# The seam of two feed-forward stages: banks, sum tiles, token low parts and planned load times

## The chip, the cores and the metric

One core of one Trainium2 chip runs the whole program. The metric is the device time of one execution in microseconds (us), given as the median of several runs. The engines are named as in the profile: PE is TensorE (its weight loads are listed as PEld), DVE is VectorE, ACT is ScalarE, POOL is GpSimd, and SP is the engine whose queue issues the DMAs here.

## The reference, cut to what matters

```python
attn_out = _attn_ref(q, k, v, f)                 # 4 batches, 8 heads, 576 tokens, 64 per head
x = attn_out.transpose(0, 2, 1, 3).reshape(2304, 512)
h = x @ moe_w_in                                 # 512 -> 2048
x = (h * (1.0 / (1.0 + np.exp(-h)))) @ moe_w_out # 2048 -> 512: the first feed-forward stage
a, b = x @ moe2_w_a, x @ moe2_w_b                # 512 -> 1536, twice
return (a * b) @ moe2_w_out                      # 1536 -> 512: the second stage
```

All of it is float32. The change concerns the end of the first stage and the whole of the second.

## The kernel before

Each float32 operand of a product is split into a high part (rounded to fp32r, by ACT) and a low part (value minus high part, by DVE or POOL). A product is then three matmuls (high by high, high by low, low by high; `mm3`, lines 336 to 338).

Weights arrive as 64-bit words and are decoded on the chip by ACT, DVE and POOL (`fields`, lines 1069 to 1078). The hidden units of a stage are cut into chunks. The second stage has six chunks, numbered j, of 256 hidden units each. Its two first products (m = 0 for `w_a`, m = 1 for `w_b`) use a Strassen-like scheme of seven products (k = 0 to 6) in the place of eight, so `matrix` makes sums and differences of weight quarters (`ws`, `stage`, line 1102), whose high and low parts go to the weight tiles `whi` and `wlo` (lines 1107 and 968 or 969). `build` does the same for the tokens: plain quarters and differences (`t`, line 1054) of the first stage's result `acc`, their high parts (line 1057) and low parts (lines 968 on DVE, 969 on POOL) into `x`.

The tokens are cut into three blocks, each of two halves of 384. A chunk is run over the three blocks; one such pass is a "third" (`third(q)`, q = 0 to 17). In a third, PE forms products `x`, `y`, `z` in PSUM, ACT and DVE combine them to `z` tiles (lines 1169 to 1200), the product a*b is split into `ghi` and `glo`, and eight second products `po` are added to `acc` (line 1221, or 1219 by ACT for j = 0). The second products of a third are placed between the first products of the next one. Where j changes, the weights of the next chunk take the place of the old ones; the text calls that a change of chunk.

The last chunk of the first stage is `finish_first`: six token blocks of two first products `ps_l`, a gate (tiles `g_l`, `ghi_l`, `glo_l`; lines 991 to 996) and four second products `po_l`, added to `acc` by DVE (line 1007). The text calls the stretch from the first `ps_l` to the first `po` of the second stage the seam.

From the seam on, the order of all engines comes from a planner. `Plan.order` takes ready operations in order of start time and priority, with a cost per operation, and an engine then executes its list strictly in that order. A buffer belongs to a tag (a ring of slots), and the buffers of one tag are taken in the order in which the program adds them, so a tile can't be taken before an older one of its tag. `plan.dma(..., late)` says how late a transfer's users are planned. An operation with `also` may be planned on a second engine, when that one would end it 0.4 us earlier than the first. The tag `u` has seven slots, for the `z` tiles and for the sums of weights and tokens alike; PSUM has the tags `s` (four banks), `t` (two), `pv` and `mm` (one each).

## Time and profile before

| | |
|---|---|
| median of 3 runs | 1018.27 us (1016.64 to 1018.53) |
| the profiled execution, own time | 1019.05 us |
| its span, first to last instruction | 1017.3 us |
| mean granted TensorE clock | 0.996 |
| the seam in it | 530.6 to 611.3 us |
| the 18 thirds of the second stage | about 580 to 1013.6 us, overlapping the seam |

The span is that of the trace; the 1.75 us between it and the execution's own time lie outside the instructions. All positions in the text are us from the span's start.

### The profile page before, as it was taken

How to read it: one execution, taken by the hardware profiler on the slowest of the kernel's cores; microseconds unless marked ns; L12 is line 12 of the kernel's file. 1: busy time of each engine (PE TensorE's matmuls, PEld its weight loads, DVE VectorE, ACT ScalarE, POOL GpSimd, SP SyncE). 2: the span in 40 equal slices, each digit the busy share in tenths (PEclk: the TensorE clock that was granted, in tenths of full speed). 3: DMA queues.
4: the chain of work that ended last, by engine and by line, in shares of the span. 5: the costliest groups of instructions: out<-in, count | busy, mean ns of one | idle time of the engine just before them, and what ended most of it. 6: DMA issues, size and time to landing. Idle time of an engine off the chain costs nothing.

```text
span 1017.3 us, 17206 instructions
## 1 busy us (share of the span) xinstructions
PE 993.3 (98%) x6041; PEld 891.5 (88%) x6041; DVE 765.5 (75%) x1854; ACT 490.5 (48%) x1211; POOL 293.1 (29%) x366
## 2 busy tenths in 40 slices
PE   8999999999999999999999989999999999999998
PEld 7667777898888888888898989999999999999998
DVE  7885656749986856757869999967887897887545
ACT  6798888955434324323325457544333334343221
POOL 5674434424322403403313232221121131130000
PEclk9999999999999999999999999999999999999999
DMA  5443333122220201201203435272262441630523
GB/s 167 147 147 112 111 101 104 58 65 70 66 63 21 82 23 32 84 11 37 89 22 125 147 136 204 73 259 83 85 215 74 154 158 63 221 110 31 195 101 109
DMA packets 64022, 105.67 MB, mean 104 GB/s; under 512 B 8764, under 2 KB 40140, under 8 KB 63904
## 3 DMA queue, kind: packets, MB, share of 16 engines
q1 hardware_dynamic: 63824, 104.13, 31.8%
q8 instruction: 47, 0.77, 0.3%
q10 hardware_dynamic: 112, 0.45, 0.2%
q14 instruction: 39, 0.32, 0.1%
HBM read 87.51 MB, written 17.03 MB: 103 GB/s over the span
## 4 chain that ended last, share of the span: by engine, by line
PE 68%; DVE 9%; DMA 1%; issue 1%; ACT 0%; SPq 0%; DVEq 0%; ACTq 0%
PE po L336 9%; PE po L337 9%; PE po L338 9%; PE ps L337 5%; PE ps L336 5%; PE ps L338 5%; PE x L336 4%; PE x L338 4%; PE x L337 4%; PE z L336 2%; PE z L338 2%; PE z L337 2%; DVE wlo L968 1%; DVE ws L1102 1%; DMA d<-in_w 1%; PE y L336 1%
## 5 line engine op out<-in xcount | busy, mean ns | idle before, releaser
L336 PE MATMUL po<-ghi,whi 128*128 128x384 f32 (+2 forms) x528 | 184.0, 352 | 4.8 <-DVE acc L1221 4.5
L337 PE MATMUL po<-glo,whi 128*128 128x384 f32 (+2 forms) x528 | 184.7, 350 | 0.0
L338 PE MATMUL po<-ghi,wlo 128*128 128x384 f32 (+2 forms) x528 | 184.7, 350 | 0.0
L336 PEld LDWEIGHTS po<-ghi,whi 128*128 128x128 f32 x528 | 99.1, 188 | 15.4 <-DVE acc L1221 7.4
L337 PEld LDWEIGHTS po<-glo,whi 128*128 128x128 f32 x528 | 99.3, 188 | 7.6
L338 PEld LDWEIGHTS po<-ghi,wlo 128*128 128x128 f32 x528 | 99.3, 188 | 7.6
L1221 DVE TENSOR_TENSOR acc<-po,acc 128x384 f32<-128x384 f32 x120 | 66.1, 551 | 51.6 <-PE po L338 51.6
L1181 ACT CAST ghi<-z 128x384 fp32r<-128x384 f32 x72 | 37.0, 514 | 115.6 <-DVE z L1177 99.7
L336 PE MATMUL x<-x,whi 128*128 128x384 f32 x264 | 89.3, 338 | 2.7 <-DVE z L1175 1.7
L1087 POOL TENSOR_TENSOR stage<-d,d 128x256 f32<-128x256 f32 x40 | 31.9, 802 | 208.3 <-DVE d L1078 116.5
L337 PE MATMUL x<-x,whi 128*128 128x384 f32 x264 | 88.9, 337 | 0.0
L338 PE MATMUL x<-x,wlo 128*128 128x384 f32 x264 | 88.8, 336 | 0.0
L337 PE MATMUL ps<-x,whi 128*128 128x512 f32 (+1 forms) x240 | 88.4, 368 | 0.0
L336 PE MATMUL ps<-x,whi 128*128 128x512 f32 (+1 forms) x240 | 88.4, 368 | 0.0
L338 PE MATMUL ps<-x,wlo 128*128 128x512 f32 (+1 forms) x240 | 88.4, 368 | 0.0
L306 POOL TENSOR_TENSOR d<-d,whi 128x256 f32<-128x256 f32 x44 | 36.8, 840 | 145.5 <-ACT whi L305 119.6
L390 DVE SCALAR_TENSOR_TENSOR acc<-po,acc 128x512 f32<-128x512 f32 (+2 forms) x120 | 63.1, 550 | 18.9 <-PE po L338 18.6
L628 ACT ACTIVATE p<-p,nm 128x384 f32<-128x384 f32 (+3 forms) x128 | 70.7, 556 | 3.6 <-DVE nm L620 3.2
L620 DVE CUSTOM_DVE_ANT_0 p<-s,maskw 128x512 f32<-128x512 f32 (+3 forms) x128 | 55.8, 484 | 13.8 <-PE t_y L670 6.4
L546 POOL TENSOR_TENSOR qkl<-qk,qkh 128x304 fp32r<-128x304 f32 x60 | 48.6, 841 | 46.4 <-DVE qkh L542 31.0
L368 ACT CAST ghi<-g 128x512 fp32r<-128x512 f32 (+1 forms) x60 | 34.5, 576 | 40.0 <-DVE g L364 40.0
L363 ACT ACTIVATE g<-ps 128x512 f32<-128x512 f32 (+1 forms) x60 | 32.9, 549 | 42.8 <-PE ps L338 42.8
(214 smaller groups left out, 2635.9 us busy)
## 6 DMA issues: line engine op xcount, KB each, us to landing
x<-cache SPq DMA_DIRECT2D x80, 384.0 KB
d<-in_w SPq DMA_DIRECT2D x116, 256.0 KB
cache<-x SPq DMA_DIRECT2D x30, 384.0 KB
qk<-in_qk SPq DMA_DIRECT2D x15, 608.0 KB
vt<-in_v SPq DMA_DIRECT2D x16, 320.0 KB
out_t<-acc SPq DMA_DIRECT2D x24, 192.0 KB
rb<-invs SPq DMA_DIRECT2D x32, 128.0 KB
d2ghi<-in_w SPq DMA_DIRECT2D x8, 256.0 KB
```

Source lines behind the costliest of these rows:

```text
L306: nc.gpsimd.tensor_sub(m, val, hi.bitcast(F32))
L336: nc.tensor.matmul(ps, wh, mh, start=start, stop=False, skip_group_check=joined)
L337: nc.tensor.matmul(ps, wh, ml, start=False, stop=False, skip_group_check=joined)
L338: nc.tensor.matmul(ps, wl, mh, start=False, stop=stop, skip_group_check=joined)
L363: nc.scalar.activation(g, ps, AF.Tanh, scale=0.5)
L368: nc.scalar.copy(ghi[:, t, :n], g)
L390: nc.vector.scalar_tensor_tensor(a, ps, 0.5, a, ALU.mult, ALU.add)
L546: plan.add("POOL", t_pool(QK // 4), lambda c=c: nc.gpsimd.tensor_sub(lo()[:, c], raw()[:, c], hi().bitcast(F32)[:, c]), [(hi, "h"), raw], ...
L620: plan.add("DVE", t_dve(nj) + 13, lambda out=out, low=low, o=o, mk=mk: nc.vector.tensor_tensor_reduce(out(), o(), mk, -SCALE, 3.0e38, ALU. ...
L628: plan.add("ACT", t_act(sum(IB[ib]), 279), lambda b=b, c=c, nj=sum(IB[ib]): nc.scalar.activation(b()[:, :nj], b()[:, :nj], AF.Exp, bias=nm ...
L1181: plan.add("ACT", t_act(N2, 93), lambda: nc.scalar.copy(ghi()[:, t, h], z()), [z], [(ghi, t, h)], at)
L1221: plan.add("DVE", t_dve(N2), lambda ps=ps, a=a: nc.vector.tensor_add(a, ps()[:, :N2], a), [ps], [key], at + 2)
```

## The change

1. The four second products `po_l` of a block take the banks `t`, `t`, `pv`, `mm` in the place of `t` alone.
2. Sums of weights and tokens get a tag of their own, `sum`, with two slots.
3. `build` offers its low parts to POOL first and to DVE second, and goes through the columns c in the outer loop and the terms k in the inner one. All seven terms of block 1 are built in one call, and block 0 is built between the two weight matrices.
4. Loads of weights and of saved tokens are planned 2.5 us later.

```diff
-    SLOTS.update(u=7, g=2)
+    SLOTS.update(u=7, g=2, sum=2)
...
-    def low_part(dst, full, high, reads, writes, pr, n, deps=()):
-        plan.add("DVE", t_dve(n), lambda: nc.vector.tensor_sub(dst(), full(), high()), reads, writes, pr, port=True,
-                 also=[("POOL", t_pool(n), lambda: nc.gpsimd.tensor_sub(dst(), full(), high()))])
+    def low_part(dst, full, high, reads, writes, pr, n, first="DVE"):
+        ways = [("DVE", t_dve(n), lambda: nc.vector.tensor_sub(dst(), full(), high())),
+                ("POOL", t_pool(n), lambda: nc.gpsimd.tensor_sub(dst(), full(), high()))]
+        if first == "POOL":
+            ways.reverse()
+        plan.add(*ways[0], reads, writes, pr, port=True, also=ways[1:])
...
-                ps = bank2("t", f"po_l{i}_{oc}")
+                ps = bank2(("t", "t", "pv", "mm")[oc], f"po_l{i}_{oc}")
...
-                    [("cache", blk, k, i)], [(key, slot)], pr + k)
+                    [("cache", blk, k, i)], [(key, slot)], pr + k, late=2500)
...
-        for k in terms:
-            for c in range(2):
+        for c in range(2):
+            for k in terms:
...
-                    src = key = temps[k, c] = tbuf("u", [P, N2], F32, f"t_{blk}_{k}_{c}")
+                    src = key = temps[k, c] = tbuf("sum", [P, N2], F32, f"t_{blk}_{k}_{c}")
...
-                low_part(lo, src, lambda hi=hi: hi().bitcast(F32), [key, ("xh", st[k], c)], [("xl", st[k])], pr + k, N2)
+                low_part(lo, src, lambda hi=hi: hi().bitcast(F32), [key, ("xh", st[k], c)], [("xl", st[k])], pr + k, N2, "POOL")
+        for k in terms:
...
-        plan.dma(480, 8 * P * QW, lambda: nc.sync.dma_start(u(raw), src.bitcast(U32)), (), [raw], pr)
+        plan.dma(480, 8 * P * QW, lambda: nc.sync.dma_start(u(raw), src.bitcast(U32)), (), [raw], pr, late=2500)
...
-                dst = temps[name] = tbuf("u", [P, QW], F32, f"w{name}_{j}_{m}")
+                dst = temps[name] = tbuf("sum", [P, N2], F32, f"w{name}_{j}_{m}")
...
-    weights(0, -400)
-    build(0, (0, 1, 2, 3, 4, 5, 6), -250)
-    build(1, (0, 1, 2, 3, 4, 5), 40)
+    weights(0, -400, lambda: build(0, (0, 1, 2, 3, 5, 4, 6), -250))
...
-            build(1, (6,), 60)
+            build(1, (0, 1, 2, 3, 5, 4, 6), 40)
```

The first place is POOL in the seam, before: ten low parts of tokens in the whole seam (`x` or `spare` from `acc` or `t`), among decode work (`stage`).

```order
208 L969 TENSOR_TENSOR x<-acc_3499,x 128x384 x2
209 L969 TENSOR_TENSOR x<-acc,x 128x384
210 L1087 TENSOR_TENSOR stage_4523<-d_1_02_6968,d_1_02_6980 128x256
211 L1087 TENSOR_TENSOR stage_4523<-d_1_03_6974,d_1_03_6985 128x256
212 L1087 TENSOR_TENSOR stage_4523<-d_1_00_7056,d_1_00_7066 128x256
213 L1087 TENSOR_TENSOR stage_4523<-d_1_01_7069,d_1_01_7082 128x256
214 L969 TENSOR_TENSOR x<-acc,x 128x384 x2
215 L969 TENSOR_TENSOR x<-t_3_0_7214,x 128x384
```

And POOL in the changed kernel, at about the same place.

```order
206 L969 TENSOR_TENSOR x<-acc_3499,x 128x384
207 L1135 TENSOR_TENSOR wlo_6581<-d_0_23_6843,d_0_23_6874 128x256
208 L969 TENSOR_TENSOR x<-t_5_0_6889,x 128x384
209 L969 TENSOR_TENSOR x<-acc_3499,x 128x384
210 L969 TENSOR_TENSOR x<-t_4_0_6921,x 128x384
211 L969 TENSOR_TENSOR x<-acc,x 128x384
212 L969 TENSOR_TENSOR x<-t_2_1_6948,x 128x384
213 L969 TENSOR_TENSOR x<-t_3_1_6960,x 128x384
```

Of the 42 low parts of tokens 10 were on POOL and 25 are there now; the other 17 are on DVE, where 32 were.

The second place is DVE where chunk 1 gives way to chunk 2 (third q = 5 to 6), before: between the additions of the second products `po_10` and `po_11` to `acc` (rows 1341 and 1356) stands a run of weight sums and low parts.

```order
1347 L1102 TENSOR_TENSOR ws_2_0_8682<-ws_2_0_8670,stage_4523 128x256
1348 L1102 TENSOR_TENSOR ws_2_1_8685<-stage_4524 128x256
1349 L1102 TENSOR_TENSOR stage_4523<-stage_4523 128x256
1350 L968 TENSOR_TENSOR wlo_6581<-ws_2_0_8670,whi_6580 128x256
1351 L1102 TENSOR_TENSOR stage_4523<-stage_4523,ws_2_0_8682 128x256
1352 L1102 TENSOR_TENSOR stage_4524<-stage_4524 128x256
1353 L968 TENSOR_TENSOR wlo_6581<-ws_2_0_8682,whi_6580 128x256
1354 L968 TENSOR_TENSOR wlo_6581<-stage_4523,whi_6580 128x256 x2
1355 L968 TENSOR_TENSOR wlo_5938<-stage_4524,whi_5937 128x256
1356 L1221 TENSOR_TENSOR acc_3499<-po_11_8660,acc_3499 128x384
```

And the same additions in the changed kernel.

```order
1334 L1227 TENSOR_TENSOR acc_3499<-po_10_8617,acc_3499 128x384
1335 L1227 TENSOR_TENSOR acc_3499<-po_11_8643,acc_3499 128x384
1336 L968 TENSOR_TENSOR glo_8559<-z_1_11_8543,ghi_8548 128x384
1337 L968 TENSOR_TENSOR wlo_6581<-stage_4523,whi_6580 128x256
1338 L1181 TENSOR_TENSOR z_0_01_8573<-z_0_8512,z_0_01_8573 128x384
1339 L1206 TENSOR_TENSOR z_1_10_8684<-z_0_10_8673,x_1_8442 128x384
1340 L968 TENSOR_TENSOR wlo_5938<-stage_4524,whi_5937 128x256
1341 L1181 TENSOR_TENSOR z_1_01_8586<-z_1_8524,z_1_01_8586 128x384
```

The weight sums of chunk 2 now stand earlier and apart from each other, in rows 1236 to 1320, so that no run of them is left between these additions.

The third place is ACT in the third q = 3, where quarters of chunk 2's weights (`d_2_10`, `d_2_11`) enter it, before: the first step on a loaded quarter (line 1070) stands between additions and casts for the third.

```order
779 L1219 COPY acc<-po_03_8102 128x384
780 L1070 ACTIVATE d_2_10_8149<-d_2_10_8100 128x256
781 L1219 COPY acc_3499<-po_10_8138 128x384
782 L1181 CAST ghi_8052<-z_1_11_8072 128x384
783 L1198 COPY z_0_10_8169<-x_0_7961 128x384
```

And the same quarters in the changed kernel.

```order
796 L1074 ACTIVATE d_2_10_8346<-d_2_10_8289 128x256
797 L1187 CAST ghi_8256<-z_1_11_8283 128x384
798 L1204 COPY z_0_10_8367<-x_0_8179 128x384
799 L1074 ACTIVATE d_2_11_8371<-d_2_11_8320 128x256
800 L1187 CAST ghi_8256<-z_1_10_8385 128x384
```

The numbers in the names rise with the planned order of the whole program: the step on `d_2_10` moved from 8149 to 8346, which is in the next third (q = 4).

## Rows read from the trace of the kernel before

**Rows 1.** The page: busy time of each engine, share of the span, instructions.

```profile
PE 993.3 (98%) x6041; PEld 891.5 (88%) x6041; DVE 765.5 (75%) x1854; ACT 490.5 (48%) x1211; POOL 293.1 (29%) x366
```

**Rows 2.** Waits of PE from 530 us on: us in total, times, longest.

```profile
PE po_l L336 <- DVE acc L1007: 6.0, 3, 2.9
PE po L336 <- DVE acc L1221: 4.5, 4, 1.4
PE x L336 <- DVE z L1175: 1.7, 1, 1.7
```

**Rows 3.** Windows: length, busy us (instructions) of PE, PEld, DVE, ACT, POOL; clock, DMA, GB/s.

```profile
580.00:600.00 20.00, 16.15 (x82) 15.35 (x81) 19.59 (x37) 10.08 (x22) 7.22 (x6) 0.91 0.44 157
600.00:620.00 20.00, 20.00 (x117) 19.77 (x116) 18.90 (x43) 12.96 (x31) 1.47 (x2) 1.00 0.53 184
```

**Rows 4.** Timeline of PE in the seam: start, us, instruction [idle before <- releaser].

```profile
543.28 0.44 PE L336 MATMUL po_l<-ghi_l,whi 128*128 128x384 f32 x1 [1.71 <-DVE acc L1007]
...
545.33 0.53 PE L336 MATMUL po_l<-ghi_l,whi 128*128 128x384 f32 x1
545.65 0.53 PE L337 MATMUL po_l<-glo_l,whi 128*128 128x384 f32 x1
...
563.45 0.45 PE L336 MATMUL po_l<-ghi_l,whi 128*128 128x384 f32 x1 [1.45 <-DVE acc L1007]
...
593.76 0.45 PE L336 MATMUL po_l<-ghi_l,whi 128*128 128x384 f32 x1 [2.86 <-DVE acc L1007]
```

**Rows 5.** Windows over the seam, and over two thirds around a change of chunk.

```profile
530.60:611.30 80.70, 73.61 (x399) 71.59 (x398) 77.12 (x160) 43.03 (x98) 26.58 (x28) 0.96 0.38 131
722.70:747.20 24.50, 23.03 (x131) 22.39 (x131) 20.50 (x50) 7.77 (x18) 4.15 (x6) 1.00 0.62 207
747.20:770.10 22.90, 22.90 (x134) 22.90 (x133) 20.70 (x48) 9.11 (x22) 8.28 (x11) 1.00 0.44 134
```

**Rows 6.** The chain that ended last, in the seam: start, us, what.

```profile
580.39 1.41 DVE t L1054 x3
...
585.07 2.93 DVE t L1054 x3
...
590.23 3.02 DVE t L1054 x3
```

**Rows 7.** Timeline of POOL in the seam.

```profile
564.01 1.19 POOL L969 TENSOR_TENSOR x<-acc,x 128x384 fp32r<-128x384 f32 x1 [2.17 <-ACT x L1057]
...
584.80 2.31 POOL L969 TENSOR_TENSOR x<-acc,x 128x384 fp32r<-128x384 f32 x2 [7.70 <-ACT x L1057]
...
589.76 2.59 POOL L969 TENSOR_TENSOR x<-acc,x 128x384 fp32r<-128x384 f32 x2
```

**Rows 8.** Timeline of DVE from 564 us.

```profile
564.25 1.11 DVE L1007 SCALAR_TENSOR_TENSOR acc<-po_l,acc 128x384 f32<-128x384 f32 x2
565.27 0.28 DVE L1072 TENSOR_SCALAR d<-d 128x256 uint32<-128x256 uint32 x1
565.47 0.42 DVE L1074 SCALAR_TENSOR_TENSOR d<-d,d 128x256 uint32<-128x256 uint32 x1
565.81 0.55 DVE L968 TENSOR_TENSOR x<-acc,x 128x384 fp32r<-128x384 f32 x1
```

**Rows 9.** Timeline of PE after the seam: the first, second and last of five stops.

```profile
670.56 0.45 PE L336 MATMUL x<-x,whi 128*128 128x384 f32 x1 [1.67 <-DVE z L1175]
...
726.34 0.44 PE L336 MATMUL po<-ghi,whi 128*128 128x384 f32 x1 [1.40 <-DVE acc L1221]
...
937.30 0.44 PE L336 MATMUL po<-ghi,whi 128*128 128x384 f32 x1 [0.33 <-DVE acc L1221]
```

**Rows 10.** Timeline of DVE before the stop at 726 us: first and last row.

```profile
719.28 0.42 DVE L1102 TENSOR_TENSOR ws<-stage 128x256 f32<-128x256 f32 x1
...
725.75 0.55 DVE L1221 TENSOR_TENSOR acc<-po,acc 128x384 f32<-128x384 f32 x1
```

**Rows 11.** Timeline of ACT before the stop at 670 us.

```profile
667.97 0.44 ACT L1070 ACTIVATE d<-d 128x256 f32<-128x256 f32 x1 [2.67 <-DMA d<-in_w]
```

More of the change, by code (lines that the diff above doesn't have):

```diff
@@ L954, in model_kernel @@
     cache = dram.tile([THIRDS, len(TERMS), 2, P, 2 * N2], F32, name="cache")
-    SLOTS.update(u=7, g=2)
+    SLOTS.update(u=7, g=2, sum=2)
     plan = Plan()
-    tags = {k: Tag(SLOTS[k]) for k in ("s", "t", "pv", "mm", "ghi", "glo", "g", "u", "d0", "d1", "d2", "d3")}
+    tags = {k: Tag(SLOTS[k]) for k in ("s", "t", "pv", "mm", "ghi", "glo", "g", "u", "sum", "d0", "d1", "d2", "d3")}
     gpool = gp[0]
     def tbuf(tag, shape, dtype, name):
-        pool = {"u": more, "s": aps, "t": aps, "pv": aps, "mm": mm}.get(tag, dpool[0] if tag[0] == "d" else gpool)
+        pool = {"u": more, "sum": more, "s": aps, "t": aps, "pv": aps, "mm": mm}.get(tag, dpool[0] if tag[0] == "d" else gpool)
         return Buf(tags[tag], lambda: pool.tile(shape, dtype, name=name, tag=tag, bufs=SLOTS[tag]))
@@ L1101, in sum_of @@
                 fd, kd = lambda: at(STAGED.index(to)), ("st", m, STAGED.index(to))
-            plan.add("DVE", t_dve(QW), lambda: op(fd(), fa(), fb()), [ka, kb], [kd], pr + 2, port=True)
-            return fd, kd
+            plan.add("DVE", t_dve(QW), lambda: op(fd()[:, :QW], fa()[:, :QW], fb()[:, :QW]), [ka, kb], [kd], pr + 2, port=True)
+            return (lambda: fd()[:, :QW]), kd
         def convert(k, src, key):
@@ L1117, in matrix, with weights @@
         convert(6, *sum_of("s4", sub, "12", "s2", to="12"))
-    def weights(j, pr):
+    def weights(j, pr, between=lambda: None):
         for m in range(2):
             matrix(j, m, pr)
+            if not m:
+                between()
         for n in range(4):
```

## The prediction

> **What bounds the kernel now.** I read the busy times first, then the waits of PE, then windows, then the timelines of the engine that PE waits for. PE is busy for 98% of the span [rows 1], so the kernel can only gain where PE stops or runs slowly. Order and code differ only from the seam on, and the waits of PE there fall into two kinds [rows 2]: second products of the first stage that wait for a PSUM bank until DVE has added the older product to `acc` (6.0 us, three times), and stops inside the second stage (4.5 us on `acc`, 1.7 us on a `z` tile).
>
> The seam loses more than its waits. Undisturbed, PE does 117 matmuls in 20 us [rows 3], 0.171 us each. The seam has 399 in 80.7 us [rows 5]; these would take 399 x 0.171 = 68.2 us, so 12.5 us are lost. Part of it is the clock: after the stop before 543.28 the steps between matmuls are 0.32 us [rows 4], and a window with such a stretch shows a granted clock of 0.91 where the next shows 1.00 [rows 3]; that is the lower of the two levels (1.2 GHz) for part of the window. What holds PE up is DVE, which is busy for 77.1 of the 80.7 us [rows 5]. In the second stage five stops are left [rows 9]: the one at 670.56, three like that at 726.34, and a short one at 937.30.
>
> **The change, part by part.**
>
> **The seam.** I count DVE's work between the first addition behind 530.8 us and the last low part that the first `po` needs, from the order of both programs. Before: 100 instructions on 384 columns, 38 on 256 columns, and 20 of the short tensor-scalar kind. After: 90, 34 and 13. Nine token low parts have gone from DVE by then, seven short and seven longer decode steps have been put off, two `z` steps fall behind the mark, and one token sum and three weight low parts have come in. From start to start a 384-column sum takes 0.47 us undisturbed (three in 1.41 [rows 6]), a 256-column step 0.34 and a short one 0.20 [rows 8]. So 47.0 + 12.9 + 4.0 = 63.9 us become 42.3 + 11.6 + 2.6 = 56.5 us: 7.4 us less.
>
> POOL takes part of that back. Three sums that take 1.41 us alone take 2.93 and 3.02 us beside two POOL low parts of 2.31 and 2.59 us [rows 6, 7]. The delay is (1.52 + 1.61) / (2.31 + 2.59) = 0.64 us per us of POOL. Two additions that read PSUM, in contrast, take 1.02 us from the first's start to the next instruction's, beside a POOL low part of 1.19 us [rows 7, 8]: 0.08 us more than twice 0.47. Over the whole seam the held-up time is 77.1 - 63.9 = 13.2 us for 26.6 us of POOL [rows 5], 0.50 per us. After, POOL has 22 low parts of tokens and 11 other steps in this stretch. At 1.19 us [rows 7] and 0.81 us (26.58 less 10 x 1.19, over the other 18 of the 28 [rows 5]) that is 35.1 us, which holds DVE for 17.5 us. DVE then needs 56.5 + 17.5 = 74.0 us in the place of 77.1. With its idle time as it is (3.6 us) the first `po` starts 3.1 us earlier.
>
> The bounds: at 0.64 the sum is 79.0 + 3.6 = 82.6 us, 1.9 us later than now; at nothing, which is near to what the PSUM additions show, DVE is done in 60.1 us, PE's own 68.2 us decide, and the gain is 12.5 us. I take 4 us: the 3.1 and a little for idle time, since DVE waits less for late loads. It is nearest to the average over the seam, because the mix of additions and sums on DVE stays much the same.
>
> **The four banks** are not a term of their own. They cost no instruction. They let PE run up to four second products ahead of DVE, so the stops at 543, 563 and 594 us go, and with them the stretch at the lower clock behind each. But the same banks `pv` and `mm` are taken next by the products `y` of the first third. Of PE's 390 matmuls ahead of the first `po` 336 stand ahead of the first `y`; undisturbed they end 336 x 0.171 = 57.5 us after 530.6, at 588. DVE has added the last `po_l` only after 48 of its 56.5 us and some 13 us of holding, near 594. I expect what is left of PE's waiting there, some 5 us in the place of the three stops.
>
> **Sum tiles.** At 726 us PE waits for an addition that DVE starts at 725.75, behind a run of weight sums and low parts that began at 719.28 [rows 9, 10]. The run stands there because the sums shared the ring `u` with the `z` tiles and had to wait for the last of these. With a ring of their own they come earlier and apart. A stop costs more than its 1.40 us: the third in which it lies takes 24.5 us for 131 matmuls [rows 5], 131 x 0.171 = 22.4, so 2.1 us. Three such stops and the short one (0.33 us idle [rows 9], some 0.9 with the slow starts behind it) are 7.2 us.
>
> **Loads planned later.** ACT waits 2.67 us for a weight load at 667.97 [rows 11], the additions and copies behind it are late, and PE stops for 1.67 us at 670.56 [rows 9]; with the slow starts 2.0 us. The step on that quarter now stands in the next third, while its load is issued about as long ahead of it as the plan says. The SP queue keeps its order of loads, fetches and saves but for a few places, and no wait of PE for a fetch shows in rows 2. Nothing else is charged for it.
>
> These two terms are 7.2 + 2.0 = 9.2 us. I take 8, since five changes of order will hardly leave no new stop. Bounds: 0 and 9.2.
>
> **The sum**: 4 + 8 = 12 us. The profiled execution would go from 1019.05 to 1007; it stands 0.8 us above the median. From the median of 1018.27 I come to 1006.3 us.
>
> **The rivals.**
>
> **A. The seam gives nothing, the rest holds.** It holds if POOL delays DVE at 0.64 and not at 0.50. For it: 15 more low parts on POOL, 1.19 us each, hold up what is left of the sums. Against it: a third of DVE's instructions there (42 of 137) read PSUM. Seam -1.9, rest 8: 1018.3 - 6.1 = 1012.2.
>
> **B. The third before a change of chunk becomes too full for DVE.** By the order it now has 57 DVE instructions, where a third of the trace has 48 in 20.70 us [rows 5]: 0.43 us each, 24.6 us in a third of 22.6 (132 x 0.171). Two us each at four changes give back 8. Against it: the next third has only 43 and an addition may be some 4 us late before PE needs its bank. Then the seam's 4 us are left: 1014.
>
> **C. Slower: POOL holds DVE for the whole of each low part.** Each of the 15 moved parts frees 0.47 us and would cost 1.19 us: 15 x 0.72 = 10.8 us longer in a seam that DVE bounds, less the 8 later: 1021. It decides from a cost of about 1.0 us per moved part on (0.47 + 8 / 15). Rows 6 and 7 show 0.76 us (1.52 / 2) at the worst place, and nothing beside PSUM additions.
> The Trainium skill says so as a rule (SBUF — State Buffer, "SBUF: two separate sides"): a DVE instruction with two operands in SBUF and a GpSimd instruction that reads SBUF take the same port pair as a lock, and the second one waits for the whole of the first. By that rule alone the sum would be rival C's. The trace agrees in kind, since the sums are held and the PSUM additions are not, but only two thirds of POOL's time is lost even where sums stand in a row.
> It also warns (Perfetto Trace Analysis, "Optimizing Scalar/DVE Operations") that offloading between these two engines "might not help"; the seam's 7.4 us that shrink to 3.1 say the same.
>
> **D. No change.** The wait only moves from the `po_l` to the `y` products, and the weight steps, however spread, end at the same moment. For it: the weight tiles are free for new parts only once the old products are done, in both programs. Time 1018.
>
> **How the numbers follow.** A measurement of this kernel tells 0.2%, some 2 us. I give the forecast 0.62, A 0.17, B 0.12, C 0.05 and D 0.04. A, B and the forecast are faster by more than that: 0.91; C is slower: 0.05; D is the same: 0.04. The range begins at 1001, where the seam gives 8 to 9 and the rest all of its 9, and ends at 1014, which takes in A and B; C and D are left out above it, and what little lies below 1001.
>
> **What the profile would show.** The three stops on `acc` at 543, 563 and 594 are gone, and the clock shows 1.00 from 540 to 580. PE waits at the first `y`, for an addition of a `po_l`. The first `po` starts near 607. POOL is busy for some 35 us in the seam, and sums on DVE take about twice as long beside it as alone. DVE's additions to `acc` no longer stand behind a run of `ws`; the stops at 670, 726, 797, 867 and 937 are gone. ACT shows fewer waits for `d<-in_w`. I am wrong if DVE, with fewer instructions, is not done earlier in the seam, or if stops of 1 to 2 us come back in each third before a change of chunk.

## The result

The changed kernel takes 1006.19 us (median of 4 runs, 1005.49 to 1006.69) beside 1017.45 us for the kernel before: a ratio of 0.989, 95% interval 0.9873 to 0.9907. Its profiled execution took 1006.17 us with a span of 1004.4 us, 12.9 us less than the span before. The code below the seam's first lines has moved: `acc` of a `po_l` is added in L1010, sums of tokens are L1057, casts L1060, loads enter at L1074, weight sums are L1106, `z` steps L1175 (ACT) and L1181 (DVE).

The busy times of the page, which answer to [rows 1]:

```profile
PE 989.3 (98%) x6041; PEld 890.1 (89%) x6041; DVE 761.0 (76%) x1851; ACT 486.6 (48%) x1211; POOL 303.2 (30%) x369
```

The waits of PE from 520 us on (us in total, times, longest), which answer to [rows 2]:

```profile
PE x L336 <- DVE z L1181: 4.5, 3, 3.7
PE x L336 <- ACT z L1175: 0.7, 1, 0.7
PE po_l L336 <- ACT ghi_l L999: 0.4, 1, 0.4
```

No wait for an addition to `acc` is left, neither in the seam nor at a change of chunk. All waits lie in the seam but for two on `z` steps soon behind it (0.55 us at 618.5 and 0.22 us at 641.9). Windows over the seam and in it (columns as in [rows 3]):

```profile
528.72:605.28 76.56, 71.70 (x392) 69.93 (x391) 70.76 (x137) 40.53 (x96) 35.87 (x32) 0.96 0.35 121
...
540.00:560.00 20.00, 20.00 (x117) 20.00 (x117) 19.39 (x36) 10.61 (x24) 12.15 (x14) 1.00 0.46 152
560.00:580.00 20.00, 19.64 (x113) 19.13 (x112) 20.00 (x42) 8.87 (x22) 7.41 (x6) 1.00 0.50 178
580.00:600.00 20.00, 15.59 (x74) 14.95 (x73) 15.93 (x29) 10.38 (x25) 11.95 (x10) 0.83 0.24 78
600.00:620.00 20.00, 19.37 (x108) 18.42 (x107) 19.36 (x38) 11.13 (x26) 7.27 (x7) 1.00 0.70 244
```

From 540 to 580 us almost nothing holds PE any more (117 and 113 matmuls in 20 us). Then come 74 in 20 us, where 117 are possible: the loss has moved to 580 to 600. The first `ps_l` now starts at 528.72 us, before at 530.62, and the first `po` at 605.28, before at 611.29. Between the two lie 76.6 us in the place of 80.7: 4.1 us less. Ahead of the first `po` stand 390 matmuls from the first `ps_l` on, before 396, so 1.0 us of this is only moved: the seam gives 3.1 us. From the first `po` to the end of the span it took 406.0 us and takes 399.1: 6.9, and with the 1.0 us that moved there 7.9. The other 1.9 of the 12.9 us between the spans arose ahead of the seam, where each engine does the same instructions in the same order in both kernels; they belong to these two executions and not to the change. What is left, 11.0 us, is near the 11.3 us between the medians.

What holds PE in the new place is seen in the chain of waits, taken at 580 to 592 us (start, us, what):

```profile
580.32 1.28 POOL stage L1091
581.61 1.41 issue
583.01 1.06 POOL stage L1091
584.07 1.28 POOL x L969
585.35 0.98 POOL spare L969
...
586.36 1.36 DVE t L1057
...
591.05 0.48 DVE z L1181
...
591.58 0.69 PE x L336
```

("Issue" is time for which the chain names no cause; the one at 581.61 lies inside the first of the two additions to `stage`, whose row stands in the last section.) POOL's two additions to `stage` take 3.75 us from start to end, where one takes 0.73 to 0.74 us undisturbed; the low parts of tokens behind them come late; DVE stands idle for 1.87 us, since its next sum needs one of the two slots of `sum`, which POOL hasn't read out; and the `z` step for which PE waits stands behind that sum and six other steps. PE stops for 3.71 us at 591.58, and its steps are 0.32 us until 597.

ACT's wait for loads of weights, before and now, in the same stretch:

```profile
ACT d L1070 <- DMA d<-in_w: 37.6, 33, 3.6
```

```profile
ACT d L1074 <- DMA d<-in_w: 1.4, 1, 1.4
```

### The profile page after: what moved, and what is told of

It is laid out like the page before. It is cut to its first block, busy times and chain, and to the rows that moved or that the text cites. A ratio compares the mean times of both kernels' runs of the same rounds, so it can differ in the third digit from the quotient of the medians.

```text
span 1004.4 us, 17192 instructions
## 1 busy us (share of the span) xinstructions
PE 989.3 (98%) x6041; PEld 890.1 (89%) x6041; DVE 761.0 (76%) x1851; ACT 486.6 (48%) x1211; POOL 303.2 (30%) x369
## 5 line engine op out<-in xcount | busy, mean ns | idle before, releaser
L390 DVE SCALAR_TENSOR_TENSOR acc<-po,acc 128x512 f32<-128x512 f32 (+2 forms) x120 | 63.1, 550 | 19.1 <-PE po L338 18.8
L336 PEld LDWEIGHTS x<-x,whi 128*128 128x128 f32 x264 | 49.8, 189 | 6.3 <-DVE z L1181 4.9
```

The lines of the kernel that those rows point to most:

```text
L336: nc.tensor.matmul(ps, wh, mh, start=start, stop=False, skip_group_check=joined)
L390: nc.vector.scalar_tensor_tensor(a, ps, 0.5, a, ALU.mult, ALU.add)
```

## The experiments

An order is planned anew for nearly every edit here: a kernel with one part left out also differs in thousands of rows. So besides the total I compare where the loss arises: the start of the n-th matmul counted from the first `ps_l`, less the start of that first, less n times 0.171 us. The second stage's first products begin near n = 260, the first `po` near 390, and n = 2663 is the last matmul. With no stop at all some 4.6 us still gather between 700 and the end (0.173 us a step, not 0.171). Each loss is read from one traced execution, and executions of one kernel differ: the four of the kernel with small DVE parts took 998.1, 998.4, 1000.6 and 1000.8 us. So where two losses differ by less than some 2 us, the column alone doesn't tell the kernels apart.

| kernel | median us | ratio to before, 95% interval | loss at n = 180 | 300 | 390 | 480 | 700 | 2663 |
|---|---|---|---|---|---|---|---|---|
| before | 1017.5 to 1017.8 | 1 | 6.3 | 6.6 | 12.9 | 13.4 | 13.9 | 27.6 |
| changed | 1006.19 | 0.9890 (0.9873–0.9907) | 0.4 | 1.5 | 9.9 | 11.0 | 12.0 | 16.6 |
| changed, no banks | 1005.07 | 0.9873 (0.9858–0.9888) | 3.2 | 5.9 | 8.3 | 9.3 | 9.8 | 14.4 |
| changed, no POOL first | 1005.21 | 0.9869 (0.9853–0.9886) | 0.4 | 2.2 | 9.1 | 9.4 | 9.9 | 14.5 |
| changed, neither | 1006.12 | 0.9884 (0.9859–0.9910) | 2.5 | 7.2 | 10.1 | 10.3 | 11.4 | 16.0 |
| changed, sums in `u` | 1017.14 | 0.9995 (0.9984–1.0006) | 0.4 | 2.1 | 3.6 | 14.1 | 14.6 | 25.9 |
| changed, early loads | 1007.60 | 0.9900 (0.9885–0.9914) | 0.8 | 2.6 | 9.0 | 9.9 | 12.8 | 17.7 |
| before + ring for sums | 1010.08 | 0.9916 (0.9897–0.9936) | 3.0 | 4.3 | 8.5 | 10.4 | 13.3 | 17.9 |
| before + banks | 1015.34 | 0.9973 (0.9963–0.9983) | 0.8 | 1.9 | 10.5 | 11.3 | 11.8 | 25.1 |
| before + late loads | 1013.18 | 0.9959 (0.9943–0.9974) | 3.6 | 4.4 | 10.2 | 10.4 | 11.5 | 23.1 |
| changed, 3 sum slots, 6 of `u` | 1008.09 | 0.9897 (0.9878–0.9916) | 0.4 | 2.2 | 9.7 | 10.3 | 11.8 | 17.5 |
| changed, small POOL parts | 996.12 | 0.9792 (0.9763–0.9821) | 0.4 | 0.7 | 0.9 | 1.1 | 2.0 | 6.6 |
| changed, small DVE parts | 999.50 | 0.9827 (0.9792–0.9863) | 0.4 | 0.7 | 3.6 | 3.8 | 4.6 | 9.2 |
| changed, Silu on ACT | 1000.90 | 0.9840 (0.9810–0.9869) | 0.4 | 0.7 | 4.5 | 4.9 | 6.4 | 11.5 |

### One part left out

**No banks.**

```diff
-                ps = bank2(("t", "t", "pv", "mm")[oc], f"po_l{i}_{oc}")
+                ps = bank2("t", f"po_l{i}_{oc}")
```

> The changed kernel with the four second products of a block back on the bank tag t alone. Theory (the banks are what removes the stops on acc in the seam; the gain behind the first po is independent of them): PE waits again on an addition to acc two or three times between 540 and 600, with a stretch of 0.32 us steps behind each; the first po starts 2 to 5 us later than 605.3; from first po to the end still about 399 us; 1008 to 1011 us. Rival (DVE's total work ahead of the first po sets the seam, so banks only move PE's waiting): the stops come back but the one of 3.7 us on a z step at 591 shrinks by as much, the first po stays within 1 us of 605.3, about 1006 us.

The waits of PE of this kernel from 520 us on:

```profile
PE po_l L336 <- DVE acc L1010: 3.8, 4, 2.1
PE x L336 <- DVE z L1181: 1.3, 2, 0.8
```

The stops on `acc` are back, and the 3.7 us at 591 are gone in exchange: 0.84 us is the longest wait on a `z` step. The loss is 3.2 us at n = 180 in the place of 0.4, and at 480 it is 9.3 in the place of 11.0. The rival holds: the banks move PE's waiting, they don't shorten it.

**No POOL first.** 12 low parts of tokens are on POOL in the place of 25 (the trace shows 12; the text before the run says 8).

```diff
-                low_part(lo, src, lambda hi=hi: hi().bitcast(F32), [key, ("xh", st[k], c)], [("xl", st[k])], pr + k, N2, "POOL")
+                low_part(lo, src, lambda hi=hi: hi().bitcast(F32), [key, ("xh", st[k], c)], [("xl", st[k])], pr + k, N2)
```

> The changed kernel with the token low parts offered to DVE first again (8 of them on POOL in the place of 25). Theory (POOL holds DVE about 0.35 us per us of POOL, as read from the changed kernel's seam): DVE gets 17 more parts of 0.47 us, 8.0 us, and is rid of 17 x 1.19 = 20.2 us of POOL, 7.1 us of holding; the first po is about 1 us later, 1006 to 1008 us. Rival 1 (POOL is nearly free for DVE, the move is the whole gain of the seam): the first po about 5 to 8 us later, 1011 to 1014 us. Rival 2 (POOL's lateness causes DVE's idle wait for a slot of the sum ring at 586 and PE's 3.7 us stop at 591): with POOL nearly empty that wait and stop vanish, the first po is 2 to 4 us earlier, 1002 to 1004 us.

The time is 1005.21 us, a little below the theory's range. The first `po` starts 76.9 us behind the first `ps_l` (76.6 in the changed kernel), with 6 more matmuls ahead of it, and the loss at 480 is 9.4. The interval overlaps with that of the changed kernel, so the move of these 13 parts is worth nothing that can be told. Rival 1, by which it was the seam's gain, falls. Rival 2 falls too: DVE's idle wait for the ring is gone, and PE still stops for 1.79 and 2.15 us on `z`.

**Sums in `u`.**

```diff
-                    src = key = temps[k, c] = tbuf("sum", [P, N2], F32, f"t_{blk}_{k}_{c}")
+                    src = key = temps[k, c] = tbuf("u", [P, N2], F32, f"t_{blk}_{k}_{c}")
...
-                dst = temps[name] = tbuf("sum", [P, N2], F32, f"w{name}_{j}_{m}")
+                dst = temps[name] = tbuf("u", [P, N2], F32, f"w{name}_{j}_{m}")
```

> The changed kernel with the sums of weights and tokens back in the ring u of the z tiles. Theory (sharing the ring makes the weight sums of the next chunk stand in a run behind the last z tile, ahead of additions to acc): stops of PE on acc of 1 to 1.5 us come back near the changes of chunk (around 720, 790, 860, 930), from first po to the end 404 to 407 us in the place of 399, total 1011 to 1014 us. Rival (the stops went because loads are planned later and the order is new; the ring does nothing): no such stops, 1005 to 1007 us.

All of the gain is gone. Two rows of PE's timeline, the longest stop of this kernel and the first of four on `acc`:

```profile
619.34 0.69 PE L336 MATMUL x<-x,whi 128*128 128x384 f32 x1 [6.25 <-ACT z L1175]
...
723.83 0.45 PE L336 MATMUL po<-ghi,whi 128*128 128x384 f32 x1 [1.40 <-DVE acc L1227]
```

The late stops are those of before to a hundredth of a us (three of 1.40 and one of 0.33), the theory's part (25.9 - 14.1 = 11.8 us between 480 and the end, in the place of 5.6: 6.2 us). The other 3.1 us I had not named: ahead of 619 DVE works through the token sums of block 1, which the shared ring has put off, and PE waits. (The other 1.6 us between the medians are not in these losses: 0.7 lie ahead of the seam, and the traced execution was 1.0 us faster than its median.) At n = 390 this kernel had lost only 3.6 us. A seam that looks good at the first `po` can still owe work that is due by n = 480, so I read all kernels there.

**Early loads.**

```diff
-                    [("cache", blk, k, i)], [(key, slot)], pr + k, late=2500)
+                    [("cache", blk, k, i)], [(key, slot)], pr + k)
...
-        plan.dma(480, 8 * P * QW, lambda: nc.sync.dma_start(u(raw), src.bitcast(U32)), (), [raw], pr, late=2500)
+        plan.dma(480, 8 * P * QW, lambda: nc.sync.dma_start(u(raw), src.bitcast(U32)), (), [raw], pr)
```

> The changed kernel with loads planned as early as before (no 2.5 us). Theory (ACT stands at the head of its queue for a load that hasn't landed, and what is behind it comes late to PE): ACT's waits for in_w are back at 30 to 40 us over the second stage, a stop of PE of 1 to 2 us comes back near 670, 1007.5 to 1009 us. Rival (ACT is busy for half the time only and its waits cost nothing): ACT's waits are back and PE shows no new stop, 1006 us within 0.5.

The wait of ACT and the new stop of PE:

```profile
ACT d L1074 <- DMA d<-in_w: 37.4, 32, 3.4
```

```profile
643.24 0.44 PE L336 MATMUL x<-x,whi 128*128 128x384 f32 x1 [1.31 <-DVE z L1181]
```

The time is in the theory's range, but its path is shown in part only. The stop comes 27 us earlier than I said, and a late load stands far ahead of it. A row of DVE, and two pieces of the chain that leads to the stop:

```profile
631.40 0.29 DVE L1076 TENSOR_SCALAR d<-d 128x256 uint32<-128x256 uint32 x1 [0.84 <-ACT d L1074]
```

```profile
639.15 1.15 DVE wlo L968
...
642.65 0.55 DVE z L1181
```

DVE idles for 0.84 us at 631.40, behind an ACT that waits for a load; from there to the `z` step it has no gap of 0.1 us. Between n = 480 and the stop it has 47 instructions, and POOL 11; up to the same matmul the changed kernel has 41 and 6, and a stop of 0.22 us. So earlier loads also bring steps on weights into this stretch, in which DVE is full. How much of the stop is due to ACT's waiting isn't shown, and 37 us of it cost this one stop at most. The total alone (1.4 us) doesn't tell the two kernels apart, since the intervals overlap; the row does.

### One part alone, and two left out

**The ring alone, on the kernel before.** The diff is that of the two `tbuf` lines above, turned round, with the tag `sum` of two slots and the changed kernel's order of columns and terms in `build` (shown in part):

```diff
-        for k in terms:
-            for c in range(2):
+        for c in range(2):
+            for k in terms:
...
-    build(0, (0, 1, 2, 3, 4, 5, 6), -250)
-    build(1, (0, 1, 2, 3, 4, 5), 40)
+    build(0, (0, 1, 2, 3, 5, 4, 6), -250)
+    build(1, (0, 1, 2, 3, 5, 4), 40)
```

> The kernel before, with the sums of weights and tokens in a ring of their own of two slots, and the columns of the tokens in the outer loop with the terms in the order of the change, without which two slots are too few. No other banks, no POOL first, no later loads. Theory (the ring of its own is what the gain consists of; taking it from the changed kernel cost 11 us): the stops on acc at 726, 797, 867 and 937 are gone, some 3 us come from the stretch up to 620 us as well; 1007 to 1010 us, what is left being the loads (1.4 us). Rival (the ring pays only together with banks that let DVE lag and POOL that takes the low parts; taking it out hurt since the new order of tokens without it is bad): the late stops go, 6 to 7 us, and the seam stays as it was, with the three stops on acc; 1011 to 1013 us.

1010.08 us, 7.8 less than before, at the theory's upper end. No stop on `acc` is left behind the seam; in it three are (2.5 us). What remains against the changed kernel is seen between n = 480 and 700: 2.9 us in the place of 1.0, with a stop of 1.58 us at 644, at the place of the one with early loads. Here ACT waits for no load between 553 and 644 us, so it is the steps on weights and not ACT's waiting that make this stop: PE waits for a `z` step of a DVE that has no gap of 0.1 us from 628 us on.

**The banks alone.**

```diff
-                ps = bank2("t", f"po_l{i}_{oc}")
+                ps = bank2(("t", "t", "pv", "mm")[oc], f"po_l{i}_{oc}")
```

> The kernel before, with the four second products of a block on the banks t, t, pv, mm. Theory (DVE's work up to about 620 us sets the seam, the banks only move the place at which PE waits): the stops at 543, 563 and 594 go, a stop of some 5 us comes ahead of the first x or y products of the second stage; the first po within 1.5 us of where it was; 1016 to 1018.5 us. Rival (the prediction's four banks take three stops and their slow stretches away): the first po 3 to 5 us earlier, 1012.5 to 1015 us.

In the seam the timeline of PE has one long stop, in the place of the three on `acc` of the kernel before:

```profile
590.78 0.69 PE L336 MATMUL x<-x,whi 128*128 128x384 f32 x1 [5.98 <-ACT z L1169]
```

At n = 180 the loss is 0.8 and not 6.3, at 480 it is 11.3 and not 13.4. That is the theory's exchange, but not quite one for one: 2.5 us are kept, and the time lies between the two ranges.

**Late loads alone.** The diff of the early loads, turned round, on the kernel before.

> The kernel before with the loads of weights and of saved tokens planned 2.5 us later, and nothing else. Theory (ACT stands behind a load that hasn't landed, which costs PE the stop at 670 and nothing else): ACT's waits for in_w fall from 37.6 us to a few, the stop at 670 is gone, the four stops on acc behind it and the seam stay, 1015.5 to 1016.5 us. Rival (the later steps on the weights then stand closer before the change of chunk, so that the stops on acc grow by as much): 1017 to 1018.5 us, with longer stops at 726, 797 and 867.

1013.18 us, a gain of 4.4, outside both. The table shows where it lies: 3.0 us ahead of n = 480 (13.4 become 10.4), in the seam that the theory left as it was, and 1.5 us behind. Behind it the stop at 670 is gone, and that one did come from a load, as the chain of the kernel before shows:

```profile
662.08 5.87 DMA d<-in_w
...
667.97 0.45 ACT d L1070
...
670.04 0.48 DVE z L1175
```

The stops on `acc` have shrunk as well, which neither theory said: the four are 0.33 to 0.38 us long, before three of them were 1.40. But five new stops of 0.28 to 0.49 us have come on an `x` (658, 662, 781, 851 and 922 us), which cost about as much as that brings:

```profile
PE po L336 <- DVE acc L1221: 1.4, 4, 0.4
PE x L336 <- DVE z L1175: 1.4, 3, 0.5
```

Why the stops on `acc` shrank stands in DVE's and POOL's timelines. First the run of weight steps in the kernel before:

```profile
719.95 0.96 DVE L1102 TENSOR_TENSOR ws<-ws,stage 128x256 f32<-128x256 f32 x1
720.84 1.23 DVE L1102 TENSOR_TENSOR ws<-stage 128x256 f32<-128x256 f32 x1
...
722.66 0.96 DVE L1102 TENSOR_TENSOR stage<-stage,ws 128x256 f32<-128x256 f32 x1
...
724.21 1.61 DVE L968 TENSOR_TENSOR wlo<-stage,whi 128x256 fp32r<-128x256 f32 x3
```

```profile
719.84 0.79 POOL L1087 TENSOR_TENSOR stage<-d,d 128x256 f32<-128x256 f32 x1 [25.23 <-DVE ws L1102]
720.59 1.20 POOL L969 TENSOR_TENSOR glo<-z,ghi 128x384 fp32r<-128x384 f32 x1
722.59 0.75 POOL L969 TENSOR_TENSOR wlo<-ws,whi 128x256 fp32r<-128x256 f32 x1 [0.80 <-ACT whi L1107]
724.70 0.84 POOL L1087 TENSOR_TENSOR stage<-d,d 128x256 f32<-128x256 f32 x1 [1.37 <-DVE wlo L968]
```

Then the same place in the kernel before with late loads:

```profile
714.41 0.42 DVE L1102 TENSOR_TENSOR ws<-ws,stage 128x256 f32<-128x256 f32 x1
714.74 1.24 DVE L1102 TENSOR_TENSOR ws<-stage 128x256 f32<-128x256 f32 x1
715.91 0.96 DVE L1102 TENSOR_TENSOR stage<-stage 128x256 f32<-128x256 f32 x1
...
718.13 1.08 DVE L968 TENSOR_TENSOR wlo<-stage,whi 128x256 fp32r<-128x256 f32 x3
```

The run is the same; it is held up in two places in the place of four, because POOL's two additions to `stage` don't fall into it any more. So some 1.05 us of each stop of 1.40 were these two POOL steps, and 0.35 are left of the run with the other two in it. The ring cures the stop by dissolving the run, the later loads by taking half of POOL's work out of it.

The parts don't add: alone they give 7.8, 4.4 and 2.5 us, 14.7 in sum, and together 11.3. By the table that lies in the seam. Behind n = 480 ring, loads and banks alone give 6.7, 1.5 and 0.4 us, 8.6 in sum, and the changed kernel gives 8.6 as well (14.2 us of loss become 5.6). Ahead of it they give 3.0, 3.0 and 2.1 us, 8.1 in sum, and the changed kernel 2.4.

**Neither banks nor POOL first.** Both diffs of above.

> The changed kernel without the two edits that were meant for the seam's engines: second products on t alone, and the token low parts offered to DVE first. What is left is the ring for sums, the order of the tokens and the later loads. Theory (each of the two cost nothing when it was left out alone, and one does not stand in for the other): 1004 to 1007 us, as fast as the changed kernel. Rival (each covers for the other: the banks give PE the slack that a loaded DVE needs, or POOL gives DVE the time that the single tag needs, so leaving both out shows what the pair is worth): 1009 to 1013 us, stops on acc in the seam of 5 us or more in total.

1006.12 us (four runs, 1004.4 to 1009.6): the theory. The gain of 11.3 us is that of the ring, with the order of tokens that goes with it, and of the later loads.

### What sets the seam

In the eight changed or half-changed kernels so far, the one with sums in `u` left out, the loss at n = 480 lies between 9.3 and 11.3 us, whatever is done with banks and POOL. Four runs ask what it is.

**Another ring.** Three slots for sums in the place of two, six of `u` in the place of seven.

```diff
-    SLOTS.update(u=7, g=2, sum=2)
+    SLOTS.update(u=6, g=2, sum=3)
```

> The changed kernel with three slots for sums and six for z tiles, in the place of two and seven. Theory (DVE stood idle for 1.87 us at 586 for a slot of the sum ring that POOL was late to read, and PE's stop of 3.7 us and the slow steps behind it came from that): the wait of DVE on POOL for t is gone, the stop at 591 is under 2 us, 1002 to 1004.5 us. Rival (POOL and DVE hold each other up whatever the ring, so the lateness comes out elsewhere; or six slots for z are too few and PE waits for z in every third): 1006 us or more.

The rival. DVE doesn't wait for a sum slot any more, the loss at 480 is 10.3 us, and PE stops all the same, for 4.29 us at 590.17 (on an ACT copy that stands behind a cast of a token sum). The wait for the ring was where the lateness showed, not where it came from.

**Small low parts.** These two keep every instruction at its place in every queue. In the first, 23 low parts of tokens on POOL are cut to 16 columns, in the second the 17 on DVE (the texts before the runs say 22 and 16; the traces show 23 and 17). `few` is 16 for all of these but the parts in `spare`; the other columns are left out.

```diff
-                ("POOL", t_pool(n), lambda: nc.gpsimd.tensor_sub(dst(), full(), high()))]
+                ("POOL", t_pool(n), lambda: nc.gpsimd.tensor_sub(dst()[:, :few], full()[:, :few], high()[:, :few]))]
...
-        ways = [("DVE", t_dve(n), lambda: nc.vector.tensor_sub(dst(), full(), high())),
+        ways = [("DVE", t_dve(n), lambda: nc.vector.tensor_sub(dst()[:, :few], full()[:, :few], high()[:, :few])),
```

> The changed kernel with 22 of the low parts of tokens that POOL makes cut to 16 of their 384 columns; the rest of these low parts is left out of the result. Every instruction of every engine stands where it stood, so that only POOL's time on these 22 changes, from about 1.2 us to a few tenths each. Theory (POOL holds DVE at 0.35 us per us, and DVE's total up to about 615 us sets the seam): some 20 us of POOL less give DVE 7 us back; the sums of DVE beside them take 0.47 us each, DVE's wait for the ring at 586 and PE's stop of 3.7 us at 591 are gone; the first po 4 to 7 us earlier, 999 to 1002 us. Rival (the seam's loss of some 10 us has another cause than DVE, which has slack that the profile shows as busy time, or POOL does not hold it): first po within 1 us of 605.3, 1005 to 1006.5 us.

> The changed kernel with the 16 low parts of tokens that DVE makes cut to 16 of their 384 columns; the rest of these is left out of the result. Every instruction stands where it stood. Theory (DVE's total sets the seam): 16 times some 0.4 us, 6 us less for DVE up to about 620 us; POOL keeps its 25 and its holding; the first po 3 to 6 us earlier, 1000.5 to 1003 us. Rival (POOL's lateness and the wait for the ring set it, so that DVE only waits longer): first po within 1.5 us of 605.3, 1004.5 to 1006.5 us.

Busy times of the page of the first, and POOL's groups in its seam (530 to 606 us; one more such part comes later):

```profile
PE 985.0 (99%) x6041; PEld 888.6 (89%) x6041; DVE 750.6 (75%) x1851; ACT 487.8 (49%) x1211; POOL 284.1 (29%) x369
```

```profile
L969 POOL TENSOR_TENSOR x<-t,x 128x16 fp32r<-128x16 f32 x13 | 5.4, 417 | 14.2 <-ACT x L1060 14.1
...
L969 POOL TENSOR_TENSOR x<-acc,x 128x16 fp32r<-128x16 f32 x9 | 3.1, 344 | 5.9 <-ACT x L1060 5.9
```

Busy times of the second:

```profile
PE 985.4 (99%) x6041; PEld 887.8 (89%) x6041; DVE 754.3 (76%) x1851; ACT 487.1 (49%) x1211; POOL 302.4 (30%) x369
```

Both theories hold, and both times lie below their ranges, by 2.9 and 1.0 us. In the first DVE has the same 1851 instructions in the same order and is busy for 10.4 us less (761.0 - 750.6), because POOL is busy for 19.1 us less (303.2 - 284.1): 0.54 us of DVE for each us of POOL. The kernel is 10.1 us faster (1006.19 - 996.12), and PE's waits from 520 us on show no entry. In the second nothing but 17 instructions of DVE has changed, and POOL is as busy as ever (302.4 us); DVE is relieved of 6.7 us (761.0 - 754.3), and the kernel is 6.7 us faster. So it is DVE's work that sets the seam, and in these two a us off DVE is a us off the kernel. Some of the time comes by way of the clock: the changed kernel's window from 580 to 600 us has a granted clock of 0.83, and these two have 1.00 from 525 to 620. It also shows why moving parts to POOL gave nothing: a whole one takes 0.47 us off DVE, and 1.19 us of POOL hold DVE for some 0.54 x 1.19 = 0.64.

**Silu on ACT.** ACT is busy for 41 of the seam's 77 us, so the gate of `finish_first` goes there whole: 12 instructions fewer on DVE, and a Silu on ACT for each Tanh.

```diff
-                plan.add("ACT", t_act(N2), lambda ps=ps, g=g: nc.scalar.activation(g(), ps()[:, :N2], AF.Tanh, scale=0.5),
+                plan.add("ACT", t_act(N2), lambda ps=ps, g=g: nc.scalar.activation(g(), ps()[:, :N2], AF.Silu),
                          [ps], [g], pr + 10 * t + 5)
-                plan.add("DVE", t_dve(N2), lambda ps=ps, g=g: nc.vector.scalar_tensor_tensor(
-                    g(), g(), 1.0, ps()[:, :N2], ALU.add, ALU.mult), [ps], [g], pr + 10 * t + 5)
...
-                    a, ps()[:, :N2], 0.5, a, ALU.mult, ALU.add), [ps], [("acc", oc, h, blk)], pr + 135 + 10 * oc)
+                    a, ps()[:, :N2], 1.0, a, ALU.mult, ALU.add), [ps], [("acc", oc, h, blk)], pr + 135 + 10 * oc)
```

> The changed kernel with the gate of finish_first by one Silu on ACT in the place of a Tanh on ACT and a scalar-tensor-tensor on DVE, and the factor 1.0 in the place of 0.5 at the addition to acc. Theory (DVE's total sets the seam; ACT has time to spare): 12 instructions of 0.47 us, 5.6 us, leave DVE; the loss up to the 480th matmul of the seam falls from some 10 to 5 or 6 us; 1000.5 to 1003.5 us, and that would be faster than both kernels. Rival (a chain through ACT and POOL sets the seam, or the new planned order is unlucky, or another function on ACT has to be loaded at a price): 1005 to 1008 us.

1000.90 us, as the theory said: 5.3 us less than the changed kernel for 12 x 0.47 = 5.6 us of work, and its interval lies below that of the changed kernel. DVE's busy time on the page falls by 2.9 us only (761.0 to 758.1): up to n = 480 it is busy for 84.0 us in the place of 85.9 and idle for 3.0 in the place of 7.1. So the us for us of the small parts is not a rule for DVE's busy time where the order changes too. The group of the new instruction in the seam, and one instruction ahead of the first:

```profile
L994 ACT ACTIVATE g_l<-ps_l 128x384 f32<-128x384 f32 x12 | 5.8, 487 | 4.0 <-PE ps_l L338 4.0
```

```profile
530.78 1.28 ACT L994 ACT_TABLE_LOAD   x1 [0.22 <-PE ps_l L338]
```

A Silu takes 487 ns; the Tanh took 484 in the same place of the changed kernel. The rival's price for another function is there too, one table load of 1.28 us at 530.78, but it costs PE nothing: the loss at n = 180 is 0.4 us with it and without. This version beats both kernels.

## Why the prediction was right, and where it was not

**The total and its two halves.** A gain of 12 us was forecast, and 11.3 us were measured. That the time itself is met to 0.1 us is luck: the median of the kernel before was 1018.27 us for the forecast and 1017.45 beside the result. Between the first `ps_l` and the first `po` the trace gives 4.1 us (4 forecast), of which 1.0 us is only moved; the rest gives 7.9 us with that (8 forecast).

**The stops behind the seam came out whole.** Behind n = 700 the kernel before loses 13.7 us, 9.1 more than the 4.6 that gather without a stop; 9.2 were forecast for its five stops. The changed kernel loses 4.6 there. The 1.2 us that the forecast took off for new stops are seen as well: between n = 390 and 700 the changed kernel loses 2.1 us and the one before 1.0.

**The seam: the right engine, and a size from terms that were off.** DVE sets it, as the run with small DVE parts shows. Its 137 instructions in the seam are the 90, 34 and 13 that were counted, and POOL is busy for 35.87 us (35.1 forecast). The price of POOL was the step with the widest bounds: 17.5 us of holding were taken, 0.50 us of DVE per us. If I add up what the 26 lengthened instructions of DVE in the seam took beyond undisturbed ones, I get 13.6 us, 0.38 per us (in the kernel before 11.5 for 26.6, 0.43, where the prediction worked out 13.2). Against that, DVE's idle time was left at 3.6 us and is 5.8 (76.56 - 70.76). The two errors have opposite signs, so the size of the seam is in part luck. The gain is not in the token parts: they are neutral, and the seam's improvement comes with any of ring, banks and late loads (11.3 to 10.4 us of loss at n = 480, before 13.4), not with their sum.

**Sums beside POOL** were to take about twice as long. Of the 19 token sums in the seam ten took 0.54 to 0.55 us, as alone, and nine 0.79 to 1.42.

**The four banks.** "Not a term of their own" is right for the changed kernel (with and without them: 1006.19 and 1005.07); alone they give 2.5 us. The clock is 1.00 from 540 to 580 as said. The step that failed is the place of the wait: I put 5 us at the first `y`, for a late addition of a `po_l`. PE waits six matmuls ahead of it, at an `x` and for a `z` step, and the additions are in time. DVE's queue holds the sums of tokens ahead of that `z` step; I had followed the banks to their next taker and not DVE's queue to its next customer.

**The ring.** 7.2 us forecast by taking each late stop at 2.1 us with what follows it; 7.8 alone, 11.0 when taken out, 6.2 of the latter at the late stops. The mechanism, a run of weight steps ahead of an addition, is seen in the rows. Its size is not the ring's own: three quarters of each long stop were two POOL steps that held that run.

**Late loads.** 2.0 us were forecast for one stop, at 670. Its chain does run through a load, and it is gone in the changed kernel and with later loads alone. Taken out of the changed kernel they are worth 1.4 us, which the intervals don't tell from nothing, and the stop that comes is another one, at 643, behind a full DVE. Alone they give 4.4 us, 3.0 of it in the seam: the term was priced by the stop that I saw and not by what the moved steps do on DVE and POOL.

**The rivals.** A needed a hold of 0.64 over the whole seam; it is 0.38 there, and 0.54 for the token parts with the order held fixed. B's third before a change of chunk has no stop. C needed 1.0 us per moved part; 23 parts made small give DVE 10.4 us, 0.45 each. In D the wait only moves; it did move, but 11.3 us remain.

The rule of the Trainium skill behind C (SBUF — State Buffer, "SBUF: two separate sides"), that the second of two such instructions waits for the whole of the first, agrees with the trace of the changed kernel. A held instruction of DVE ends a fixed time behind the end of POOL's, as the last section shows, so the two thirds that the prediction read against the rule don't speak against it: POOL's 1.2 to 1.3 us there include waits of POOL's own, since undisturbed it takes 1.01 us. What C had wrong is the price. DVE loses what is left of a POOL step when it comes to it, and its instructions that read PSUM lose nothing.

The warning of the Trainium skill (Perfetto Trace Analysis, "Optimizing Scalar/DVE Operations"), that offloading between the two "might not help", is borne out by the run without POOL first: 25 or 12 parts on POOL, 1006.19 and 1005.21 us.

## What to carry to other kernels

Where an engine is full for a stretch, count its instructions up to the last point at which its debts are due, not to the first milestone: banks, rings and offers to another engine moved PE's stops from 543 to 591 or 619 us and took 2 to 4 of 13.4 us of loss away, and only work taken off DVE removed the rest. Price an offload to POOL at what POOL takes back from DVE; here that was all of it, while ACT, which was busy for half of the stretch, could take 12 instructions for one table load of 1.28 us. To test which engine sets a stretch, shrink its instructions and leave every queue in order: the time follows, or it doesn't. And before a difference of two traces is split among causes, compare them where the two programs are still the same.

## What the hardware showed that was not expected

In these traces DVE and POOL hold each other up to the end of the other's instruction. Some rows of the changed kernel:

```profile
580.32 2.73 POOL L1091 TENSOR_TENSOR stage<-d,d 128x256 f32<-128x256 f32 x1 [12.92 <-DVE d L1082]
583.01 1.06 POOL L1091 TENSOR_TENSOR stage<-d,d 128x256 f32<-128x256 f32 x1
...
586.29 1.01 POOL L969 TENSOR_TENSOR x<-t,x 128x384 fp32r<-128x384 f32 x1
```

```profile
581.90 0.55 DVE L1057 TENSOR_TENSOR t<-acc,t 128x384 f32<-128x384 f32 x1
582.49 0.98 DVE L1057 TENSOR_TENSOR t<-acc 128x384 f32<-128x384 f32 x1
583.40 0.54 DVE L1010 SCALAR_TENSOR_TENSOR acc<-po_l,acc 128x384 f32<-128x384 f32 x1
583.87 0.62 DVE L968 TENSOR_TENSOR x<-acc,x 128x384 fp32r<-128x384 f32 x1
...
586.36 1.36 DVE L1057 TENSOR_TENSOR t<-acc,acc 128x384 f32<-128x384 f32 x1 [1.87 <-POOL spare L969]
```

The sum at 586.36 ends at 587.72, 0.42 us behind POOL's end at 587.30; the low part at 583.87 ends at 584.49, 0.42 behind POOL's 584.07; the addition at 583.40, which reads PSUM, takes its 0.54 us in the middle of a POOL instruction. It is so throughout: from 520 us on 22 two-operand instructions (TENSOR_TENSOR) of DVE on 384 columns in SBUF are lengthened by more than 0.06 us, and all end 0.41 to 0.42 us behind the end of a POOL instruction; 16 on 256 columns end 0.28 to 0.29 us behind one; and of 17 that read PSUM while a POOL instruction ended none is lengthened. Instructions of one operand are held as well: 1.02 us for 0.28 at 588.63.

So the price is not a share of POOL's time. A sum on DVE that comes just behind POOL's start loses 0.8 to 0.9 us (0.55 become up to 1.42), one that comes near its end nothing, and an average such as 0.38 or 0.54 holds for one order of the queues.

It goes both ways. On 384 columns POOL takes 1.01 us undisturbed and up to 1.45 beside DVE. Of the 23 low parts that were cut to 16 columns eight took 0.22 us, and the others, which waited for DVE, 0.38 to 0.65. The longest hold is the addition at 580.32: 2.73 us, where 0.73 is usual. Five instructions of DVE with both operands in SBUF ran on without a gap beside it, and POOL ended 0.60 us behind the fifth, when DVE had paused for 0.04 us. Elsewhere POOL mostly gets its turn behind the first; why not here, no run tells.
